# A recurrent attention and a bilinear network on one core: transposing keys and queries two slots at a time

## The chip, the core and the metric

The kernel runs on one core of a Trainium2 chip. The core has a matrix engine (TensorE, in the profile PE, with its weight loads as PEld), a vector engine (VectorE, DVE), a scalar engine (ScalarE, ACT), a general engine (GpSimd, POOL) and an engine that here only issues DMA transfers (SyncE, SP). Sixteen DMA engines move the data that they ask for. Each engine executes its own list of instructions in order and waits on semaphores for the others. The metric is the device time of one execution in microseconds; lower is better.

## What is computed

```python
def _attn_ref(q, k, v):                        # q, k, v: [4, 8, 768, 64] float32
    gamma = 1.0 - 2.0 ** (-5.0 - np.arange(H, dtype=np.float32))
    scale = 1.0 / np.sqrt(D)
    for t in range(S):
        state = gamma[None, :, None, None] * state + np.einsum('bhd,bhe->bhde', k[:, :, t], v[:, :, t])
        y[:, :, t] = scale * np.einsum('bhd,bhde->bhe', q[:, :, t], state)
...
    x = attn_out.transpose(0, 2, 1, 3).reshape(B * S, H * D)      # [3072, 512]
    a = x @ w_a                                # w_a, w_b: [512, 1536]
    b = x @ w_b
    return (a * b @ w_out)                     # w_out: [1536, 512]
```

A recurrence with a decay per head goes over 768 positions of 4 batches and 8 heads; its result, 3072 rows of 512, goes through two products whose outcomes are multiplied element by element and through a third product.

## The kernel before

**Slots.** The recurrence is worked in chunks of 128 positions, so that it becomes matrix products: inside a chunk, scores of queries against keys under a mask, and across chunks a state per head. One chunk of one batch, with all 8 heads, is a slot: 24 slots, numbered 0 to 23, 6 to a batch. Two neighbours (2u and 2u + 1) are a pair. The 3072 rows then go through the network in row groups of 4, 2, 2, 2, 2, 4 and 8 slots (`TILES`), whose index in the code is J.

**What happens to keys and queries.** The keys and queries of a slot are loaded in float32 (raw tiles `kf`, `qf`; values are `vf`), multiplied by a table that holds the decay, and written as bf16 into `kqb[t]`, a tile of 128 positions by 2 x 4 x 2 x 64 elements: first keys, then queries, 1,024 elements or 256 KB in all. `scaled` (L317 to L335) does one of the two halves in one instruction of 512 elements a partition. The state's products (L433) read keys from `kqb` as they are; scores (L415) and the products of queries with the state (L453) need them with the head's dimension on the partitions, as `kqT`.

**Two ways to `kqT`.** The first three pairs (slots 0 to 5) are transposed on TensorE (`flip2`, L524) and are worked by functions of their own (names that end in 2). The pairs from slot 6 on go through `flip`: a DMA transpose, issued by SP, from `kqb[t]` into one half of a tile `kqT` that belongs to the pair. There are 18 of these, of 256 KB each. In the later pairs the positions of a pair are interleaved: a score of either slot takes its keys from its own half of `kqT` and its queries from both halves (L416, L417).

**The order of the work.** `seq` (L103) chains the instructions of each engine in the order in which the program names them, so the order on each engine is the written one, and a wait holds up all that stands behind it on that engine. Semaphores between engines are put in by the framework, from the regions of the tiles that instructions read and write. A slot's preparation is `casts(t)` (L342): two scalings on GpSimd, the cast of the values where `t` isn't in 12 to 19, then on SP the transpose (L352) and, behind it, the loads for slot t + 2. For some slots the order of loads differs (L350 to L371): at t = 18 the keys and queries of slot 20 are loaded ahead of the transpose and the keys of 21 behind it. `casts_two` (L391) does this for slots 6 and 7, `late_kq` (L380) for the last four; `late_kq(20)` has the loads of slots 22 and 23 behind the two transposes. `turn(new, old)` (L477) is the attention's work on TensorE: the state and the scores of the pair `new`, the outputs of the pair `old`. Between turns TensorE works the network: `ffn_a` (L619) and `ffn_g` (L631) for the two first products, and the third product either directly (L656) or in seven products of half blocks in place of eight (`Group`, L717, with matmuls at L739). For the latter GpSimd or VectorE first forms sums of quarters of `ht` (`hsum`, L696, by the helper `tt` at L672): the tiles `hs` 1 to 4. `Group.p7` uses `hs` 3, `p6` uses `hs` 2, `p5` uses 1 and `p3` uses 4. `single(J)` (L835) works the seven products of row group J between the first blocks of the next one.

**The program around the change.** At the stretch that the prediction looks at longest, the written order is: `casts(13)`, `single(2)`, `casts(14)` with pieces of weight sums between its two scalings, blocks of row group 3, `casts(15)`, `hsum(3, 3, 0, 6)` on GpSimd, more blocks, `hsums(3, 0, 3)`, `turn(12, 10)`, blocks, `hsums(3, 3, 6)`, `casts(16)`, `single(3)`.

**Tiles.** The pool `nat` has 6 buffers of each of its tags. `kqb` is one of them: 6 slots are held at once, and the seventh waits for the readers of the first. When all slots are through, the same buffers take the sums `XS` of the last row group's input (`x_sum`, L881, on VectorE), four tiles of the same size: 3 and 2 are made first, later 1 and 4. `kqT` has 3 buffers of a pair. `load_slot` (L117) puts two slots' keys into one raw tile, and loads each slot's half by itself; for queries it loads both slots in one transfer at the even slot (L122).

Of the kernel before, what the change touches and what calls it, by code (L numbers as in the profile page):

```python
# [10 lines left out]
BF16 = mybir.dt.bfloat16  # L11
# [20 lines left out]
def kernel(  # L32
# [11 lines left out]
    P = 128  # L44
    B, H, S, D = q.shape
    NCH = S // P
    HP = H // 2
# [19 lines left out]
    nat = ctx.enter_context(tc.tile_pool(name="nat", bufs=6))  # L67
    tra = ctx.enter_context(tc.tile_pool(name="tra", bufs=4))
# [34 lines left out]
    def seq(bi):  # L103
        ins = bi.ins
        prev = last.get(ins.engine)
        if prev is not None:
            tc.add_manual_dep(ins, prev.name, nosync, reason="program order")
        last[ins.engine] = ins
        return bi
# [79 lines left out]
    kqb = {}  # L189
    kqb = {}  # L190
# [116 lines left out]
    kb, qb, vb, kqT, aT = {}, {}, {}, {}, {}  # L307
# [9 lines left out]
    def scaled(eng, t, i):  # L317
# [16 lines left out]
            tab = tab.rearrange("p (r hp) o -> p r hp o", r=2).to_broadcast([P, 2, HP, D])  # L334
        seq(eng.tensor_tensor(dst, src, tab, op=ALU.mult))  # L335

    def new_nat(t):
        kqb[t] = nat.tile([P, 2, HP, 2, D], BF16, tag="kqb", name="kqb")
        kb[t], qb[t] = kqb[t][:, 0], kqb[t][:, 1]
        vb[t] = nat.tile([P, H, D], BF16, tag="vb", name="vb")  # L340

    def casts(t, between=lambda: None):  # L342
        new_nat(t)
        scaled(nc.gpsimd, t, 0)
        between()
        scaled(nc.gpsimd, t, 1)
        if t not in range(12, 20):
            cast(nc.gpsimd, vb[t], raws["v", t])
        u = t + 2
        if u == 20:  # L350
            load_slot(u, "kq")
        flip(t)  # L352
        if u == 20:
            load_slot(u + 1, "k")
            return
        if u == 21:
            load_slot(u - 1, "v")
            load_slot(u, "v")
            load_slot(22, "kq")
            return  # L360
        if u in V_LATE:
            if u == 13:
                load_slot(12, "q")
            elif u == 19:
                load_slot(18, "kq")
            load_slot(u, {12: "k", 18: ""}.get(u, "kq"))
            if u % 2:
                load_slot(u - 1, "v")
                load_slot(u, "v")
        elif u < NSLOT:  # L370
            load_slot(u)  # L371

    def flip(t):
        if t % 2 == 0:
            kqT[t // 2] = tra.tile([P, 2, 2, HP, P], BF16, tag="kqT", name="kqT", bufs=3)
        seq(nc.sync.dma_start_transpose(
            out=kqT[t // 2][:, t % 2].rearrange("p a b c -> p (a b) c"),
            in_=kqb[t].rearrange("p a hp r d -> p (a hp r d)")))

    def late_kq(t):  # L380
        for u in (t, t + 1):
            new_nat(u)
            scaled(nc.gpsimd, u, 0)
            scaled(nc.gpsimd, u, 1)
            flip(u)
        if t == 20:
            load_slot(23, "k")
            load_slot(22, "v")
            load_slot(23, "v")

    def casts_two(t):  # L391
        for u in (t, t + 1):
            new_nat(u)
            scaled(nc.gpsimd, u, 0)
            scaled(nc.gpsimd, u, 1)
            flip(u)
        for u in (t, t + 1):
            cast(nc.gpsimd, vb[u], raws["v", u])
        load_slot(t + 3)
# [271 lines left out]
    def tt(dst, x, y, op, eng=nc.vector):  # L671
        seq(eng.tensor_tensor(dst, x, y, op=op))  # L672
# [175 lines left out]
    WS, XS, pieces = {}, {}, []  # L848
# [29 lines left out]
    def xq(k, c):  # L878
        return xt[BIG, c][:, 2 * k : 2 * k + 2]

    def x_sum(n):  # L881
        XS[n] = nat.tile([P, 2, 4 * P], BF16, tag="kqb", name=f"xs{n}")
        x, y, op = {3: (xq(1, 1), xq(0, 1), ALU.subtract), 2: (XS.get(3), xq(0, 0), ALU.add),
                    1: (xq(0, 1), xq(0, 0), ALU.subtract), 4: (xq(1, 0), XS.get(2), ALU.subtract)}[n]
        tt(XS[n], x, y, op)
# [191 lines left out]
    def big():  # L1077
        made = {"A": Group(5, 0, ST, AT0, FF), "B": Group(5, 1, FF, AT1, ST)}
        made.update({f"u{u}.": Unit(u) for u in range(2 * NP)})
        made.update(a=Group(BIG, 0, Y0, AT0, ST), b=Group(BIG, 1, Y1, AT1, FF),  # L1080
                    c=Group(BIG, 2, FF, AT0, ST, "kqT"), d=Group(BIG, 3, FF, AT1, FF, "kqT"))
        order = START.split()
        at = {7 * u + o: f"u{u}.{x}" for u in range(2, 2 * NP) for x, o in STEP.items()}
        at = [at[t] for t in sorted(at) if at[t] not in order]
        order += [x for x in at[: at.index(f"u{2 * NP - 1}.1")]] + END.split()
        for x in order:
            if x == "T":
                turn(None, 22)
            elif x[0] == "X":
                x_sum(int(x[1]))  # L1090
            elif x[0] == "S":
                hsum((BIG, int(x[1])), int(x[2]), 0, NP)
            elif x[-1] in "<>":
                made[x[:-2]].p1(*((0, NP - 1) if x[-1] == "<" else (NP - 1, NP)))
            else:
                getattr(made[x[:-1]], "p" + x[-1])()
# [226 lines left out]
```

## Time and profile before

| | |
|---|---|
| Median of 3 runs | 217.86 us (217.77 to 217.90) |
| Profiled execution | 218.26 us |
| its span | 216.6 us |
| GpSimd's two scalings of a slot | 1.04 us each (median of 40: 1,042 and 1,043 ns) |
| DMA transposes | 18, 4.5 us from issue to landing (median) |
| Key loads of one slot | 18 of 256 KB, 4.9 us from issue to landing (median) |
| Query loads of two slots | 9 of 512 KB, 5.8 us |
| Moved in all | 39.68 MB in 82,906 packets |

The span runs from the first to the last instruction that the profiler recorded; the execution's time is measured around it. A row of a timeline gives the start in us from the span's start, the length in us, the engine, the line of the code, the operation, the tile written and the tiles read, how many instructions were merged, and in brackets how long the engine had been idle and what ended that. For SP the length is the time that the queue was held by issuing the transfer; the transfer itself goes on behind it, and "to landing" counts from the start of the issue to the last piece of data that is in place. A row of the chain of waits has start, length, engine, tile and line. Engine names that end in q are an engine's queue.

### The profile page before, as it was taken

To read this page: it belongs to the slowest core of one execution; us is meant where nothing else is said; L and a number is where in the kernel's file an instruction comes from. 1 tells how busy PE (TensorE), PEld (TensorE's weight loads), DVE (VectorE), ACT (ScalarE), POOL (GpSimd) and SP (SyncE) were. 2 spreads that over 40 slices of the span, in tenths; PEclk is the share of its full clock that TensorE was granted. 3 is DMA by queue.
4 is the path that set the end of the run, shared out by engine and by line. 5 is a ranking of instruction groups with operands and counts; after the bars stand their busy time and mean duration, and the time that the engine had idled before them with its cause. 6 is when DMAs were issued, how large, how long until landed. Compare 5 with 4: busy or idle time off the path is not lost.

```text
span 216.6 us, 5726 instructions
## 1 busy us (share of the span) xinstructions
PE 209.8 (97%) x2250; PEld 145.8 (67%) x2250; DVE 151.1 (70%) x277; ACT 105.1 (49%) x236; POOL 155.5 (72%) x187
## 2 busy tenths in 40 slices
PE   7789999999999999999999999999999999999994
PEld 3458445587458888888888877557864444458883
DVE  5796347845985486356377978686577887688952
ACT  3175325343224444464576475657545656652331
POOL 7277877778889487979959979799996999530000
PEclk9999999999999999999999999999999999999999
DMA  6999999999999999399989999980013000000055
GB/s 181 315 337 370 377 360 357 363 237 240 227 267 235 173 254 280 76 189 257 213 187 227 222 200 215 236 139 3 5 73 122 0 0 3 2 0 0 27 194 170
DMA packets 82906, 39.68 MB, mean 183 GB/s; under 512 B 57536, under 2 KB 75840, under 8 KB 82880
## 3 DMA queue, kind: packets, MB, share of 16 engines
q1 hardware_dynamic: 82736, 39.26, 74.4%
q8 instruction: 17, 0.28, 0.5%
q10 hardware_dynamic: 144, 0.07, 0.1%
q14 instruction: 9, 0.07, 0.1%
HBM read 28.31 MB, written 6.29 MB: 160 GB/s over the span
## 4 chain that ended last, share of the span: by engine, by line
PE 91%; SPq 3%; DMA 3%; POOL 0%; issue 0%; DVE 0%
PE a L619 18%; PE g L631 18%; PE mA L739 12%; PE uA L913 10%; PE mB L739 6%; PE o L656 5%; PE uB L913 5%; DMA wsta<-in_moe_w_a_dram 3%; PE mC L739 3%; PE at L415 2%; PE uC L913 2%; SPq L150 2%; PE y L463 2%; PE st L433 2%; PE fa L1003 2%; SPq L138 1%
## 5 line engine op out<-in xcount | busy, mean ns | idle before, releaser
L633 DVE TENSOR_TENSOR ht<-g,asb 128x256 bf16<-128x256 f32 (+1 forms) x70 | 34.4, 493 | 30.3 <-PE g L631 27.1
L619 PE MATMUL a<-xt,wa_bf 128*128 128x256 bf16 (+1 forms) x280 | 48.6, 300 | 0.2 <-POOL wa_bf L287 0.2
L631 PE MATMUL g<-xt,wb_bf 128*128 128x256 bf16 (+1 forms) x280 | 48.4, 300 | 0.0
L622 ACT CAST asb<-a 128x256 bf16<-128x256 f32 (+1 forms) x70 | 30.0, 428 | 33.5 <-PE a L619 31.3
L631 PEld LDWEIGHTS <-wb_bf 128*128 128x128 bf16 x280 | 27.1, 98 | 10.2
L619 PEld LDWEIGHTS <-wa_bf 128*128 128x128 bf16 x280 | 26.5, 98 | 10.8 <-POOL wa_bf L287 0.6
L920 ACT COPY snap<-uA 128x512 f32<-128x512 f32 x36 | 20.0, 587 | 15.4 <-PE uA L913 13.9
L335 POOL TENSOR_TENSOR kqb<-kf,ktab 128x512 bf16<-128x512 f32 x22 | 22.9, 1045 | 5.3 <-DMA kf<-in_k_dram 4.9
L739 PEld LDWEIGHTS <-hs 128*128 128x128 bf16 x234 | 22.8, 98 | 3.6
L421 DVE TENSOR_TENSOR aT<-at,mask 128x512 bf16<-128x512 f32 x36 | 22.3, 683 | 0.3
L335 POOL TENSOR_TENSOR kqb<-qf,qtab 128x512 bf16<-128x512 f32 x18 | 19.8, 1100 | 2.6 <-DMA qf<-in_q_dram 1.6
L672 POOL TENSOR_TENSOR ht<-gsb,asb 128x512 bf16<-128x512 bf16 x13 | 15.2, 1174 | 7.5 <-DVE gsb L672 7.4
L746 ACT COPY snaps<-mA 128x256 f32<-128x256 f32 x30 | 11.0, 374 | 18.9 <-PE mA L739 18.9
L672 POOL TENSOR_TENSOR hs<-ht 128x384 bf16<-128x384 bf16 (+3 forms) x14 | 15.8, 1130 | 5.7 <-DMA kf<-in_k_dram 3.2
L739 PEld LDWEIGHTS <-ht 128*128 128x128 bf16 x180 | 17.5, 98 | 3.3
L672 POOL TENSOR_TENSOR hs<-ht,hs 128x384 bf16<-128x384 bf16 (+1 forms) x17 | 16.8, 993 | 2.5 <-DVE ht L633 2.3
L739 PE MATMUL mA<-wsum,hs 128*128 128x256 bf16 x120 | 15.2, 273 | 0.0
L672 DVE TENSOR_TENSOR osb<-mB,snaps 128x256 f32<-128x256 f32 x20 | 8.4, 422 | 8.2 <-ACT snaps L746 4.3
L287 POOL CAST vb<-vf 128x512 bf16<-128x512 f32 x12 | 7.8, 668 | 5.2 <-DMA vf<-in_v_dram 5.2
L656 PE MATMUL o<-wo_bf,ht 128*128 128x512 bf16 x48 | 10.7, 379 | 0.0
L672 DVE TENSOR_TENSOR gsb<-uB,snap 128x512 bf16<-128x512 f32 x12 | 8.2, 686 | 2.9 <-ACT snap L920 2.1
L672 DVE TENSOR_TENSOR asb<-uB,snap 128x512 bf16<-128x512 f32 x12 | 8.2, 685 | 2.9 <-ACT snap L920 2.0
(148 smaller groups left out, 379.8 us busy)
## 6 DMA issues: line engine op xcount, KB each, us to landing
out_dram<-osb SPq DMA_DIRECT2D x21, 256.0 KB, 3.9
kf<-in_k_dram SPq DMA_DIRECT2D x18, 256.0 KB, 4.9
qf<-in_q_dram SPq DMA_DIRECT2D x9, 512.0 KB, 5.8
vf<-in_v_dram SPq DMA_DIRECT2D x18, 256.0 KB, 5.1
wsta<-in_moe_w_a_dram SPq DMA_DIRECT2D x6, 512.0 KB, 7.2
wsto<-in_moe_w_out_dram SPq DMA_DIRECT2D x6, 512.0 KB, 8.7
wstb<-in_moe_w_b_dram SPq DMA_DIRECT2D x5, 512.0 KB, 7.9
kf<-in_k_dram SPq DMA_DIRECT2D x3, 512.0 KB, 7.4
```

Source lines behind the costliest of these rows:

```text
L335: seq(eng.tensor_tensor(dst, src, tab, op=ALU.mult))
L421: seq(nc.vector.tensor_tensor(aT[t][:, r], at[r], mask.to_broadcast([P, HP, P]), op=ALU.mult))
L619: seq(nc.tensor.matmul(a, wa_bf[:, kt, fs], xcols(J, kt, c0, c1), start=(kt == 0), stop=(kt == KT - 1)))
L622: seq(nc.scalar.copy(asb, a))
L631: seq(nc.tensor.matmul(g, wb_bf[:, kt, fs], xcols(J, kt, c0, c1), start=(kt == 0), stop=(kt == KT - 1)))
L633: seq(nc.vector.tensor_tensor(ht[J][:, ft, c0:c1], g, asbs.pop((J, ft, c0)), op=ALU.mult))
L656: seq(nc.tensor.matmul(o, ht[J][:, ft, i * P : (i + 1) * P], wo_bf[:, ft], start=(ft == 0), stop=(ft == NFT - 1), skip_group_check=True))
L672: seq(eng.tensor_tensor(dst, x, y, op=op))
L739: seq(nc.tensor.matmul(m, w, right[:, j], start=(first and j == 0), stop=(j == NP - 1), skip_group_check=True))
L746: seq(nc.scalar.copy(self.snaps[:, n], self.bank["A"]))
L913: seq(nc.tensor.matmul(m, w, right[:, k], start=(first and k == 0), stop=(k == 1), skip_group_check=True))
L920: seq(nc.scalar.copy(self.snaps[n], self.bank["A"]))
```

## The change

`kqb` becomes one tile for two neighbouring slots, allocated at the even slot, with 3 buffers in place of 6 of half the size; `kqb[t]` is then the slot's half of it, and what reads and writes it is unchanged. `flip` does nothing for an even slot. For the odd slot it issues one transpose of the whole pair, 128 positions by 2,048 elements, 512 KB, into the whole `kqT` tile. Slots 0 to 5 use the new tile too, but not `flip`. The four `XS` tiles become two tiles of two, in the same buffers.

```diff
+    both = {}
+
     def new_nat(t):
-        kqb[t] = nat.tile([P, 2, HP, 2, D], BF16, tag="kqb", name="kqb")
+        if t % 2 == 0:
+            both[t // 2] = nat.tile([P, 2, 2, HP, 2, D], BF16, tag="kqb", name="kqb", bufs=3)
+        kqb[t] = both[t // 2][:, t % 2]
         kb[t], qb[t] = kqb[t][:, 0], kqb[t][:, 1]
         vb[t] = nat.tile([P, H, D], BF16, tag="vb", name="vb")
...
     def flip(t):
         if t % 2 == 0:
-            kqT[t // 2] = tra.tile([P, 2, 2, HP, P], BF16, tag="kqT", name="kqT", bufs=3)
+            return
+        u = t // 2
+        kqT[u] = tra.tile([P, 2, 2, HP, P], BF16, tag="kqT", name="kqT", bufs=3)
         seq(nc.sync.dma_start_transpose(
-            out=kqT[t // 2][:, t % 2].rearrange("p a b c -> p (a b) c"),
-            in_=kqb[t].rearrange("p a hp r d -> p (a hp r d)")))
+            out=kqT[u].rearrange("p t a b c -> p (t a b) c"),
+            in_=both[u].rearrange("p t a hp r d -> p (t a hp r d)")))
...
     def x_sum(n):
-        XS[n] = nat.tile([P, 2, 4 * P], BF16, tag="kqb", name=f"xs{n}")
+        if n in (3, 1):
+            XS["pair"] = nat.tile([P, 2, 2, 4 * P], BF16, tag="kqb", name=f"xs{n}", bufs=3)
+        XS[n] = XS["pair"][:, int(n in (2, 4))]
```

## The prediction

> **What bounds the kernel now.** I read the page's busy times first, then the busy time by stages, then the transposes by themselves (when each is issued, when it lands, when TensorE first reads it), and last what GpSimd and the DMA queue wait for.
>
> ```profile
> span 216.6 us, 5726 instructions
> PE 209.8 (97%) x2250; PEld 145.8 (67%) x2250; DVE 151.1 (70%) x277; ACT 105.1 (49%) x236; POOL 155.5 (72%) x187
> ...
> 16.00:45.00 29.00, 28.82 (x299) 17.09 (x300) 17.87 (x30) 12.54 (x26) 22.31 (x31) 1.00 1.08 359
> 45.00:150.00 105.00, 104.98 (x1333) 80.67 (x1332) 73.03 (x137) 53.57 (x130) 88.08 (x96) 1.00 1.02 206
> 150.00:213.00 63.00, 63.00 (x442) 40.21 (x441) 48.02 (x78) 32.01 (x66) 36.17 (x37) 1.00 0.11 41
> ```
>
> The first two lines are the page's, the other three the busy time by stages (length, then PE, PEld, DVE, ACT, POOL, granted clock, DMA share, GB/s). From 16 to 213 us TensorE is idle for 0.18 + 0.02 + 0.00 = 0.20 us, at the full granted clock. All DMA transposes lie between 50 and 145 us, so inside a stretch in which TensorE never waits: whatever the change makes faster elsewhere can return 0.2 us at most, and whatever it makes TensorE wait for is added to the end in full, since the 63 us behind 150 have no idle time to give back.
>
> The profiled execution took 218.26 us, 1.66 more than its span; the median of the runs is 217.86, 0.40 less. I work out differences in the profiled execution and add them to 217.86.
>
> **What one transpose costs now.** All 18 together, then three stretches that hold two neighbours each (transposes of slots 6 and 7, 20 and 21, 22 and 23), and slots 16 and 17, each with its landing:
>
> ```profile
> L376 SPq DMA_TRANSPOSE kqT<-kqb x18: 1232/1332/3293, 50.3 to 141.0; - x18
> DMA to landing us min/median/max: 3.0/4.5/6.0
> ...
> L376 SPq DMA_TRANSPOSE kqT<-kqb x2: 1245/2269/3293, 50.3 to 53.7; - x2
> DMA to landing us min/median/max: 3.2/4.3/5.3
> ...
> L376 SPq DMA_TRANSPOSE kqT<-kqb x2: 1232/1232/1232, 105.9 to 108.0; - x2
> DMA to landing us min/median/max: 3.0/3.1/3.1
> ...
> L376 SPq DMA_TRANSPOSE kqT<-kqb x2: 1748/2261/2774, 130.1 to 132.9; - x2
> DMA to landing us min/median/max: 3.7/4.6/5.6
> ...
> L376 SPq DMA_TRANSPOSE kqT<-kqb x2: 1354/1781/2208, 138.4 to 141.0; - x2
> DMA to landing us min/median/max: 4.2/5.0/5.8
> ```
>
> The first row of a couple gives the time that SP is held by the instruction (ns, min/median/max), and the first and last start. Unhindered, 256 KB hold SP for 1.23 us and land 3.0 us after the start. In a backlog a second 256 KB lands 0.9 us behind the first (130.1 + 5.6 = 135.7, then 132.9 + 3.7 = 136.6). No row shows 512 KB in one transpose.
>
> **The change, part by part.**
>
> *Nine transposes go, nine double.* On SP it removes the transposes of the even slots and makes those of the odd slots cover both. The hold of SP for 512 KB lies between 1.23 us (it doesn't grow with size) and 2 x 1.23 = 2.46 us (it is all per byte); A plain load of 256 KB holds SP for 0.58 (row at 89.97 below); were that the fixed part of a transpose too, 512 KB would hold it for 0.58 + 2 x 0.65 = 1.88. I take 2.46, the price of the two instructions that the rows do show. The landing lies between 3.0 us after the start (the second half rides along) and 53.7 + 3.2 - 50.3 = 6.6 us (two, one behind the other, from the first's start); I take the odd slot's own landing plus 1.1, between the 0.9 of the backlog and the 1.23 of the hold.
>
> The Trainium skill, page "DMA: Bandwidth & Descriptors", section "Why a DMA increments its semaphore by 16 and not by 1", has a table by which generations before trn3 pushed a transpose tile by tile, so that its issue grows with its size. By that the hold is 2.46 and the stall found below is 0.32 in place of 0.19; the two equal holds of 1.23 above are one size only, and can't tell.
>
> *Does TensorE get the pair in time?* It needs both slots of a pair anyway: a score of either slot reads the queries of both (L417). So only the later transpose counted before, and nothing is lost by holding the earlier one back. The odd slots' issues on SP, then the first reads by TensorE (chain of waits):
>
> ```profile
> 63.28 2.10 SPq L376 DMA_TRANSPOSE kqT<-kqb  x1
> 71.95 1.25 SPq L376 DMA_TRANSPOSE kqT<-kqb  x1
> 88.69 1.23 SPq L376 DMA_TRANSPOSE kqT<-kqb  x1
> 89.97 0.58 SPq L129 DMA_DIRECT2D kf<-in_k_dram  x1
> 93.31 2.20 SPq L376 DMA_TRANSPOSE kqT<-kqb  x1
> 98.98 2.20 SPq L376 DMA_TRANSPOSE kqT<-kqb  x1
> 125.08 1.23 SPq L376 DMA_TRANSPOSE kqT<-kqb  x1
> ...
> 60.76 0.57 PE at L415 x32
> 76.15 0.55 PE at L415 x16
> 80.62 0.66 PE at L415 x32
> 96.74 0.57 PE at L415 x32
> 110.23 0.57 PE at L415 x32
> 116.27 0.66 PE at L415 x32
> 133.25 0.57 PE at L415 x32
> 140.27 0.57 PE at L415 x32
> 146.93 0.57 PE at L415 x32
> ```
>
> From issue to first read, pair by pair (issues of slots 7, 17, 21, 23 from the rows of couples): 60.76 - 53.7 = 7.1; 76.15 - 63.28 = 12.9; 8.7; 96.74 - 88.69 = 8.1; 11.3; 116.27 - 108.0 = 8.3; 8.2; 140.27 - 132.9 = 7.4; and for the last pair 146.93 - 141.0 = 5.9. Against the upper landing of 6.6 only the last pair is short, by 0.7 us; with the value I take, 4.2 + 1.1 = 5.3, it is 0.6 us early. So: nothing, at 0 to 0.7.
>
> *What stands behind the doubled transposes on SP.* The loads of an even slot's turn move up by the removed transpose (1.23 us or more), and those of an odd slot's turn move back by the growth of the one ahead of them, 0 to 1.23 us. Earlier loads end no wait of TensorE. Later ones matter where GpSimd waits for them and TensorE for GpSimd. GpSimd's work around two such places, and TensorE's weight loads behind the first:
>
> ```profile
> 87.62 1.04 POOL L335 TENSOR_TENSOR kqb<-qf,qtab 128x512 bf16<-128x512 f32 x1
> 88.62 1.04 POOL L335 TENSOR_TENSOR kqb<-kf,ktab 128x512 bf16<-128x512 f32 x1
> ...
> 94.91 1.04 POOL L335 TENSOR_TENSOR kqb<-kf,ktab 128x512 bf16<-128x512 f32 x1 [1.50 <-DMA kf<-in_k_dram]
> ...
> 100.36 1.78 POOL L672 TENSOR_TENSOR hs<-ht,hs 128x384 bf16<-128x384 bf16 x2
> ...
> 130.09 1.04 POOL L335 TENSOR_TENSOR kqb<-qf,qtab 128x512 bf16<-128x512 f32 x1
> ...
> 138.73 1.04 POOL L335 TENSOR_TENSOR kqb<-kf,ktab 128x512 bf16<-128x512 f32 x1 [1.11 <-DMA kf<-in_k_dram]
> ...
> 102.73 0.64 PEld L739 LDWEIGHTS <-hs 128*128 128x128 bf16 x6
> ```
>
> The key load of slot 15 (issue 89.97) stands right behind the transpose of slot 13 (88.69), which keeps its start, as GpSimd's scaling of slot 13 sets it (end 87.62 + 1.04 = 88.66). GpSimd waits 1.50 us for this load, then works without a gap: slot 15's two scalings, then the sums of ht (L672) for row group 3's product. The second of the two sums at 100.36 ends at 102.14; it is the second half of hs 2, and the weight loads of p6 need it from the fourth of six on, 102.73 + 3 x 0.107 = 103.05. The slack is 0.91 us. The load comes later by 0.9 (the data of 256 KB more ahead of it) to 1.23 (the hold); I take 1.1, so TensorE stalls 1.1 - 0.91 = 0.19 us, in a range of 0 to 0.32. (Below nothing isn't to be had: the start is GpSimd's, and more data stands ahead.) The sums behind it have the same lateness and later uses, so the stall is paid once.
>
> The key load of slot 23 (GpSimd waits until 138.73) stood behind the transposes of 20 and 21, issued from 130.1 to 132.9 + 1.75 = 134.7. The joint one can start when slot 21 is scaled, at 130.09 + 1.04 = 131.1, and is through at 133.6 (unhindered) to 134.7 (as before): the load comes up to 1 us earlier or where it was, and with it the last pair. Credit nothing.
>
> *Tiles.* kqb goes from 6 buffers of one slot to 3 of a pair. Slot 14's scaling now waits for the readers of slots 8 and 9 in place of 8 alone; both were read in the turn at 76.15, and the scaling of slot 14 begins at 88.62: 12 us of cover, and about as much for the others. The x sums (L882) take the same places in the same order. All at nothing; if the cover were gone, GpSimd would wait for the next turn.
>
> **Sum.** 9 x 1.23 us of SP's time saved at the even slots and 9 x 1.23 spent at the odd: 0 on the path. Last pair: 0. Slot 15's keys: +0.19. Span 216.6 + 0.19 = 216.8; beside the median, 217.86 + 0.19 = 218.05, say 218.1.
>
> **The rivals.**
>
> *All hidden.* The slack of 0.91 covers the later load, if the hold has a fixed part of 0.58 like a load's and the queue is empty: 217.86. Against: the data still stands ahead.
>
> *Slower: the joint transpose is blocked in its issue, and the keys of slot 15 come late.* The holds of 2.20 at 93.31 and 98.98 show that a transpose can wait 0.97 us longer in SP when others are under way; with twice as much to push, the one at 88.69 may meet this. Then it holds 2.46 + 0.97, the key load is 2.20 late, and TensorE stalls 2.20 - 0.91 = 1.29: 219.15. It decides from a lateness of 0.91 + 0.43 on. For: the hold grows with what is outstanding. Against: the two holds of exactly 1.23 at 105.9 and 108.0, and that of 88.69 itself, met no such wait.
>
> *Slower: the last pair is late.* Landing after 6.6 from 141.0 is 147.6, 0.67 after the first read: 218.53. For: it is the shortest lead, and landings reach 6.0 with half the data. Against: the queue ahead is short of loads there.
>
> *Faster.* Nine completions fewer and earlier loads give back idle time: 0.2 us at most by the stages, 217.66. More than 0.43 would need something no row shows. The Trainium skill's page "DMA: Bandwidth & Descriptors", section "Rules for kernel authors", tells to merge small transfers into one large; by it the time should fall, and here the rows cap that at 0.2.
>
> *It doesn't do what it says:* the 512 KB go out as two pieces back to back; then the hold is 2.46 and the figures are those of the forecast's upper end, 218.18.
>
> **How the numbers follow.** About 0.2% (0.43 us) is what a measurement of this kernel tells from no change. Forecast (stall 0.1 to 0.4) 0.44; all hidden 0.10; two pieces 0.02; these are "same": 0.56. Blocked issue 0.24 and last pair 0.14 are "slower": 0.38. Faster by over 0.2%: 0.06. The range goes from 217.6 (all of the 0.2 returned) to 219.2 (the blocked issue's price); a second wait of 0.97 on top is left out.
>
> **What would show it.** Right: nine transposes on SP with a hold near 2.46; TensorE's idle time between 16 and 213 us grown by 0.1 to 0.4, all of it ahead of the weight loads of hs near 103 us, with GpSimd's scaling of slot 15 about 1.1 us later than 94.91. Wrong: a gap ahead of the first reads of kqT (the last pair's above all), a hold far from 2.46, GpSimd waiting elsewhere, or TensorE as full as before and the end moved nonetheless.

## The result and the profile after

| | changed | before | ratio, 95% interval |
|---|---|---|---|
| first series, 7 runs each | 218.88 us | 217.90 us | 1.0048 (1.0027 to 1.0069) |
| again (e5), 12 and 35 runs | 218.57 us | 218.07 us | 1.0008 (0.9980 to 1.0036) |
| a third time (e10), 12 and 29 runs | 218.40 us | 218.28 us | 1.0006 (0.9996 to 1.0017) |

Times are medians. The ratios leave out executions in a slower state, which both kernels show now and then at a lower granted clock (0.976 in e10's longest, of 222.60 us), so they are not the quotients of the medians. The change is slower in the first series. In the two later ones the medians stand on the same side (+0.50 and +0.12 us) and the intervals include no change, though all 12 runs of e5 took 218.23 us or more. The first profile is of an execution of 219.82 us, the longest of its series, so it shows the loss at its largest. The page's first lines and the busy time by stages of the changed kernel (columns as before the change):

```profile
span 218.1 us, 5682 instructions
PE 209.4 (96%) x2238; PEld 145.7 (67%) x2250; DVE 150.4 (69%) x277; ACT 105.2 (48%) x236; POOL 156.1 (72%) x187
...
16.00:45.00 29.00, 28.64 (x299) 16.80 (x297) 16.69 (x28) 12.28 (x25) 21.57 (x30) 1.00 1.08 360
45.00:150.00 105.00, 103.26 (x1315) 79.33 (x1319) 72.02 (x135) 52.41 (x128) 85.87 (x94) 1.00 1.00 206
```

Between 45 and 150 us TensorE is now idle for 1.74 us, where it was idle for 0.02. (1.41 us of that is the wait shown next. The rest stands at no wait; 12 of the 2,250 matmul records are missing in this trace.) What TensorE waited for, in us in all, times, longest, and its rows around that place:

```profile
PE at L421 <- DMA kqT<-kqb: 1.4, 1, 1.4
...
140.23 0.64 PE L421 MATMUL at<-kqT 64*64 64x128 bf16 x32
...
145.93 1.03 PE L637 MATMUL g<-xt,wb_bf 128*128 128x512 bf16 x4
148.37 0.64 PE L421 MATMUL at<-kqT 64*64 64x128 bf16 x32 [1.41 <-DMA kqT<-kqb]
```

One wait, ahead of the first read of the last pair (slots 22 and 23). The same two reads in the kernel before:

```profile
140.20 0.64 PE L415 MATMUL at<-kqT 64*64 64x128 bf16 x32
146.86 0.64 PE L415 MATMUL at<-kqT 64*64 64x128 bf16 x32
```

From the first read of slots 20 and 21 to that of 22 and 23 it is 6.66 us before and 8.14 after: 1.48 us lost, all here, since at the first of these reads the two traces stand within 0.03 us of each other. In the other two profiles of the changed kernel the same distance is 7.84 (e5) and 6.92 (e10), so 1.18 and 0.26 lost: the place is the same each time and the size isn't.

**Where it comes from.** SP's rows of the changed kernel, then those of the kernel before that have not been shown:

```profile
125.12 3.03 SPq L382 DMA_TRANSPOSE kqT<-kqb  x1
128.26 1.16 SPq L129 DMA_DIRECT2D vf<-in_v_dram  x2
129.47 2.60 SPq L129 DMA_DIRECT2D kf<-in_k_dram  x1
132.12 1.03 SPq L138 DMA_DIRECT2D qf<-in_q_dram  x1
133.26 4.14 SPq L382 DMA_TRANSPOSE kqT<-kqb  x1
137.44 0.58 SPq L129 DMA_DIRECT2D kf<-in_k_dram  x1
...
144.06 1.76 SPq L382 DMA_TRANSPOSE kqT<-kqb  x1
```

```profile
119.87 2.63 SPq L376 DMA_TRANSPOSE kqT<-kqb  x1
...
127.67 1.28 SPq L129 DMA_DIRECT2D kf<-in_k_dram  x1
129.00 0.96 SPq L138 DMA_DIRECT2D qf<-in_q_dram  x1
130.06 4.62 SPq L376 DMA_TRANSPOSE kqT<-kqb  x2
134.74 0.57 SPq L129 DMA_DIRECT2D kf<-in_k_dram  x1
```

Read from the top: slot 18's 256 KB, issued at 119.87 before, now go out with slot 19's at 125.12, and that transpose holds SP for 3.03 us where slot 19's alone held it for 1.23 (+1.80). The key load of slot 22 behind it is held for 2.60 instead of 1.28 (+1.32). So the transposes of 20 and 21 begin 3.2 us later, at 133.26. Being one, they are 0.5 us quicker than the two were, and the key load of slot 23 behind them goes out at 137.44 instead of 134.74, 2.7 us late. These rows say where the time went and not which merged pair is to blame for the longer holds: e6 below shows that the pairs ahead of slot 18 have a part in them. GpSimd (its rows in the changed kernel) waits for that load:

```profile
95.89 1.04 POOL L335 TENSOR_TENSOR kqb<-kf,ktab 128x512 bf16<-128x512 f32 x1 [2.44 <-DMA kf<-in_k_dram]
...
101.35 1.78 POOL L678 TENSOR_TENSOR hs<-ht,hs 128x384 bf16<-128x384 bf16 x2
...
141.99 1.04 POOL L335 TENSOR_TENSOR kqb<-kf,ktab 128x512 bf16<-128x512 f32 x1 [3.33 <-DMA kf<-in_k_dram]
```

Slot 23 is scaled from 141.99, not 138.73; the last transpose starts at 144.06, not 141.0. All nine transposes, and the last one alone with its landing:

```profile
L382 SPq DMA_TRANSPOSE kqT<-kqb x9: 1671/3034/5332, 51.1 to 144.1; - x9
DMA to landing us min/median/max: 4.3/5.7/7.3
...
L382 SPq DMA_TRANSPOSE kqT<-kqb x1: 1761/1761/1761, 144.1 to 144.1; - x1
DMA to landing us min/median/max: 4.3/4.3/4.3
```

It lands 4.3 us after its issue; slot 23's 256 KB alone took 4.2. The lead of the last pair was 146.93 - 141.0 - 4.2 = 1.7 us; it starts 3.1 us late and takes 0.1 longer: 1.5 us are missing, the loss.

### The profile page after: what moved, and what is told of

The parts are those of the page before. It is cut to its first block, busy times and chain, and to the rows that moved or that the text cites. A ratio compares the mean times of both kernels' runs of the same rounds, so it can differ in the third digit from the quotient of the medians.

```text
span 218.1 us, 5682 instructions
## 1 busy us (share of the span) xinstructions
PE 209.4 (96%) x2238; PEld 145.7 (67%) x2250; DVE 150.4 (69%) x277; ACT 105.2 (48%) x236; POOL 156.1 (72%) x187
## 4 chain that ended last, share of the span: by engine, by line
PE 80%; DMA 8%; SPq 5%; issue 3%; POOL 2%; ACT 1%; DVE 0%; ACTq 0%; POOLq 0%
PE a L625 15%; PE g L637 15%; PE mA L745 12%; PE uA L921 9%; PE mB L745 6%; PE o L662 5%; PE uB L921 4%; DMA wsta<-in_moe_w_a_dram 3%; PE mC L745 3%; DMA qf<-in_q_dram 2%; PE uC L921 2%; DMA kqT<-kqb 2%; PE at L421 2%; SPq L150 2%; SPq L129 2%
## 5 line engine op out<-in xcount | busy, mean ns | idle before, releaser
L625 PE MATMUL a<-xt,wa_bf 128*128 128x256 bf16 (+1 forms) x277 | 48.4, 299 | 0.4 <-POOL wa_bf L287 0.2
L625 PEld LDWEIGHTS <-wa_bf 128*128 128x128 bf16 x280 | 26.5, 98 | 10.8 <-POOL wa_bf L287 0.5
L285 ACT CAST gst<-st 128x256 bf16<-128x256 f32 x14 | 5.2, 373 | 10.4 <-PE st L439 10.4
```

The lines of the kernel that those rows point to most:

```text
L625: seq(nc.tensor.matmul(a, wa_bf[:, kt, fs], xcols(J, kt, c0, c1), start=(kt == 0), stop=(kt == KT - 1)))
```

## The experiments

Two readings of this wait were to be told apart. Theory Q (queue): the key load of slot 23 stands on SP behind joint transposes and comes late, and everything behind it. Rival S (size): 512 KB in one piece land too late, whatever stands ahead. All have the kernel before on the same chip beside them; the changed kernel itself ran beside e6 to e8 (as e5) and beside e9 and e11 (as e10), but not beside e1 to e4, where the traces have to decide.

**e1: the key load moved ahead.** In `late_kq(20)` of the changed kernel:

```diff
             scaled(nc.gpsimd, u, 1)
+            if u == 21:
+                load_slot(23, "k")
             flip(u)
         if t == 20:
-            load_slot(23, "k")
             load_slot(22, "v")
```

> The changed kernel, with the key load of slot 23 issued on SP ahead of the joint transpose of slots 20 and 21 instead of behind it. Theory Q (queue: the key load of slot 23 stands behind joint transposes that hold SP, so slot 23 is scaled late and the last joint transpose is issued at 144.1 instead of 141.0): the key load is issued near 133.3 instead of 137.4, the last joint transpose near 141.0, it lands near 145.3, TensorE doesn't wait at its first read (146.9), time 217.8 to 218.1. Rival S (size: 512 KB in one piece land too late for the first read, whatever stands ahead): a stall of 0.5 us or more stays, 218.4 to 218.9. Rival W (the DMA engines have too much to move there, so the order on SP only passes the delay on): the transpose of slots 20 and 21 now lands after 140.2 and TensorE waits there, 0.2 to 0.8 us.

218.25 us against 218.13 (ratio 1.0010, 0.9985 to 1.0035). SP's rows, the scaling of slot 23's keys on GpSimd, the last transpose's landing and the first read:

```profile
132.17 1.33 SPq L129 DMA_DIRECT2D kf<-in_k_dram  x1
133.62 3.63 SPq L382 DMA_TRANSPOSE kqT<-kqb  x1
139.66 3.57 SPq L382 DMA_TRANSPOSE kqT<-kqb  x1
...
137.59 1.04 POOL L335 TENSOR_TENSOR kqb<-kf,ktab 128x512 bf16<-128x512 f32 x1
...
DMA to landing us min/median/max: 5.6/5.6/5.6
...
146.68 0.64 PE L422 MATMUL at<-kqT 64*64 64x128 bf16 x32
```

The load goes out 5.3 us earlier than in the changed kernel and GpSimd doesn't wait for it; the joint transpose starts at 139.66, lands at 145.3, and TensorE doesn't wait (no idle time stands at its row). Nine joint transposes of 512 KB are all still there. That contradicts S. The transposes of 20 and 21 are not late either (no wait at their read), so the order on SP didn't pass the delay on: they land at 133.62 + 5.6 = 139.2, and their first read is at 140.01.

**e2, e3, e4: one pair apart.** `flip` with an exception for one pair (9 in e2, 10 in e3, 11 in e4):

```diff
     def flip(t):
+        u = t // 2
+        if u in (9,):
+            if t % 2 == 0:
+                kqT[u] = tra.tile([P, 2, 2, HP, P], BF16, tag="kqT", name="kqT", bufs=3)
+            seq(nc.sync.dma_start_transpose(
+                out=kqT[u][:, t % 2].rearrange("p a b c -> p (a b) c"),
+                in_=kqb[t].rearrange("p a hp r d -> p (a hp r d)")))
+            return
         if t % 2 == 0:
             return
-        u = t // 2
```

> The changed kernel, with slots 18 and 19 transposed apart as before, all other pairs jointly. Theory Q, with the hold of SP by the joint transpose of 18 and 19 (3.03 us where the later of the two alone took 1.23) as its start: the key load of slot 23 is issued 1.5 us or more earlier than 137.4, the stall ahead of the last pair's first read falls from 1.5 to 0.3 us or less, time 217.8 to 218.2. Rival S (size of the last transpose): unchanged, 218.6 to 218.9.

> The changed kernel, with slots 20 and 21 transposed apart, all other pairs jointly. Both transposes stand at the same place of SP's queue, behind the loads of slot 22. Theory Q with its start at slots 18 and 19: the key load of slot 23 is issued at 137.4 within 0.5 us, the stall stays between 1.0 and 1.6, time 218.5 to 219.0. Theory Q with its start at the joint transpose of 20 and 21 itself: the load is issued 1 us or more earlier and the stall falls under 0.5, below 218.3. Rival S: unchanged, 218.6 to 218.9.

> The changed kernel, with slots 22 and 23 transposed apart, all other pairs jointly: the last transpose moves 256 KB and is still issued when slot 23 is scaled. Theory Q: it is issued near 144 and lands 3.0 to 4.2 us later, at 147.1 to 148.2; the stall stays between 0.3 and 1.4, time 218.2 to 218.8. Rival S: the stall goes, 217.8 to 218.0.

Against 218.13 us before, e2 took 218.15 (1.0005, 0.9985 to 1.0025), e3 218.50 (1.0010, 0.9990 to 1.0030), e4 218.75 (1.0024, 0.9997 to 1.0051). The key load of slot 23 and the last transpose in e2, then in e3:

```profile
135.40 0.58 SPq L129 DMA_DIRECT2D kf<-in_k_dram  x1
141.44 1.95 SPq L389 DMA_TRANSPOSE kqT<-kqb  x1
```

```profile
136.36 0.57 SPq L129 DMA_DIRECT2D kf<-in_k_dram  x1
142.30 2.06 SPq L389 DMA_TRANSPOSE kqT<-kqb  x1
```

In e2 no wait is left, as Q says for its start at 18 and 19. The load is out 2.0 us earlier, but this execution ran 0.8 us ahead (its first read of the last pair is at 146.06 and not 146.86), so it is 1.2 by the same clock, short of the 1.5 expected. e3 came between what it was to tell apart: the load is out 1.1 us earlier, and no wait is left in its profile, but the median stays 0.37 above, a difference that the interval doesn't tell from none. Taking either pair apart ends the wait in its profile, so the expectation of e3 that one of the two alone decides it was wrong. What e4's TensorE waits for, and its two last transposes:

```profile
PE mA L752 <- POOL hs L685: 0.2, 1, 0.2
...
L382 SPq DMA_TRANSPOSE kqT<-kqb x2: 1231/1624/2016, 140.8 to 143.2; - x2
DMA to landing us min/median/max: 3.2/3.9/4.6
```

With the last pair apart, slot 23's 256 KB start at 143.2 and land 3.2 us later at 146.4, ahead of the read: the small piece does win back what the late load cost there. In this Q was wrong: it had a wait of 0.3 to 1.4 us left at that read, and there is none. But the loss doesn't go, where S had expected it to. The late scaling of slot 23 holds up GpSimd's sums behind it, and the products that read them (at 151.4) wait instead: the products after these start at 152.65, 0.35 us later than in e3 (152.30), and the median is 0.62 above the kernel before, with an interval that just includes no change. So the late key load has two followers, the last transpose and the sums; S's remedy covers only one.

**e5, e10: the changed kernel again.**

> The changed kernel once more, on one chip with the next three. In its first profile TensorE waited 1.5 us ahead of the last pair's first read; that execution was its longest. If that wait is the whole loss, this profile shows a wait there that is equal to the excess of its span over 216.6 within 0.2 us, and the median is 0.5 to 1.2 us above the kernel before.

> The changed kernel, on one chip with the kernel with key load 23 moved. Theory Q: its median is 0.4 us or more above that of the next kernel.

The median rule held in e5, barely (+0.50). The rule on the span failed: TensorE waited 1.12 us, while the span of 217.3 is only 0.7 longer, since this execution reached the pair before already 0.5 us earlier (its row is at 139.68, not 140.20). The start of the program varies by such amounts (its first row of L625 begins at 15.57, the same products in the kernel before at 16.18); distances within one trace are the safer measure. e10's distance to e11 was 0.31 us, under the 0.4 expected. Its profile shows a second wait, on the weight loads of hs, which the other two lack:

```profile
102.98 0.32 PEld L745 LDWEIGHTS <-hs 128*128 128x128 bf16 x3
103.49 0.22 PEld L745 LDWEIGHTS <-hs 128*128 128x128 bf16 x3 [0.19 <-POOL hs L678]
```

**e6, e9: joint in one part only.** e6 has the exception for pairs 9, 10 and 11 (joint up to slot 17), e9 for all but 11 (joint only for the last).

> The changed kernel with slots 18 to 23 transposed apart as before, and the six pairs 6 to 17 jointly. Theory Q: the joint transposes of the early pairs cost nothing, the key load of slot 23 is issued near 134.7 as in the kernel before, no wait at the last pair: equal to the kernel before within 0.2%. If the early pairs cost something (slot 15's keys, 0 to 0.3 us), 0.1 to 0.3 us more, at the weight loads of hs near 103 us.

> The changed kernel with only the last pair transposed jointly, slots 6 to 21 apart as before, so that what stands ahead of slot 23's key load on SP is as before and only the last transpose is large. Theory Q: the joint transpose is issued near 141.0, lands near 145.3, TensorE doesn't wait at the last pair's first read: equal to the kernel before within 0.2%. Rival S: a wait of 0.5 us or more there, 218.4 or more.

e6: 218.10 against 218.07 (0.9996, 0.9972 to 1.0020); six joint transposes of the early pairs cost no time. But the key load of slot 23 did not go out near 134.7. Its row in e6, and the first read of slots 20 and 21:

```profile
136.04 0.57 SPq L129 DMA_DIRECT2D kf<-in_k_dram  x1
...
139.69 0.64 PE L428 MATMUL at<-kqT 64*64 64x128 bf16 x32
```

From the load to that read it is 3.65 us, where the kernel before has 140.20 - 134.74 = 5.46. So the load is 1.8 us late with no joint transpose from slot 18 on; TensorE doesn't wait, as the slack of the last pair still covers it. The same distance is 5.24 in e9, 4.00 in e2, 3.86 in e3, 3.46 in e10, and 2.75 to 2.79 in e5 and the first profile of the changed kernel. A wait at the last pair shows only in the last three: 0.19 us in e10, and 1.12 and 1.41 in the two with the shortest distance. By these traces, one of each run, the lateness gathers along the queue from the early pairs on; how much each pair adds was not separated.

e9: 218.22 against 218.28 (0.9999, 0.9988 to 1.0009). Its SP rows, the landing, the first read and the stage:

```profile
134.97 0.57 SPq L129 DMA_DIRECT2D kf<-in_k_dram  x1
141.36 1.69 SPq L389 DMA_TRANSPOSE kqT<-kqb  x1
...
DMA to landing us min/median/max: 4.3/4.3/4.3
...
146.87 0.64 PE L428 MATMUL at<-kqT 64*64 64x128 bf16 x32
...
45.00:150.00 105.00, 104.98 (x1334) 80.67 (x1332) 70.48 (x137) 53.56 (x130) 87.21 (x96) 1.00 1.03 206
```

This is the sharpest test of S: the last 512 KB go out in one piece, the load ahead is in time, and TensorE is as full as before the change. They land at 141.36 + 4.3 = 145.7, 1.2 us ahead of the read.

**e7, e8: the load's place in the kernel before.** No joint transposes; the key load of slot 23 ahead of the transposes of 20 and 21 (e7), or behind the value loads (e8, whose edit this is):

```diff
         if t == 20:
-            load_slot(23, "k")
             load_slot(22, "v")
             load_slot(23, "v")
+            load_slot(23, "k")
```

> The kernel before, with all 18 transposes, and the key load of slot 23 issued ahead of the transposes of slots 20 and 21. Theory Q: TensorE has no idle time to return there, so equal to the kernel before within 0.2%; the key load lands some 3 us earlier and the transpose of slot 23 is issued near 139.

> The kernel before, with all 18 transposes of 256 KB, and the key load of slot 23 issued behind the value loads of slots 22 and 23 instead of ahead of them: the suspected cause alone, without a joint transpose. Theory Q: the load lands 1.5 to 2.5 us later than 138.7, the transpose of slot 23 is issued as much later, and what exceeds the lead of 1.7 us is lost: 0 to 0.8 us at the last pair's first read or at the products that wait for GpSimd's sums behind slot 23; time 218.0 to 218.8. Rival S (512 KB in one piece): nothing, within 0.2% of the kernel before.

e7: 218.34 against 218.07 (1.0017, 0.9985 to 1.0049), no difference shown, as expected; the transpose of slot 23 went out at 140.1 and not near 139. e8: 219.04 against 218.07 (1.0040, 1.0006 to 1.0073), more than expected. The load, GpSimd and TensorE's waits in e8:

```profile
136.37 0.92 SPq L129 DMA_DIRECT2D kf<-in_k_dram  x1
...
142.24 1.04 POOL L335 TENSOR_TENSOR kqb<-kf,ktab 128x512 bf16<-128x512 f32 x1 [4.69 <-DMA kf<-in_k_dram]
...
PE mA L739 <- POOL hs L672: 0.8, 1, 0.8
PE at L415 <- DMA kqT<-kqb: 0.6, 1, 0.6
```

With 18 transposes of 256 KB, the late load alone makes a loss of the changed kernel's kind: GpSimd starts slot 23 at 142.24, 3.5 us late, and TensorE waits at the last pair (0.6) and at the sums (0.8). The load is issued 1.6 us later than in the kernel before, and with the value loads now ahead of it it also takes 5.8 us to land instead of 3.9. Six of its twelve executions lie at 218.06 to 218.38 and six at 219.70 to 220.30; the profile is of an upper one, so for the lower half no loss is shown. What decides between the two was not found.

**e11: the moved load again, beside the changed kernel.**

> The changed kernel with the key load of slot 23 ahead of the joint transpose of slots 20 and 21, on one chip with the changed kernel. Theory Q: 0.4 us or more below the changed kernel's median, and within 0.2% of the kernel before.

218.09 against 218.40 for the changed kernel and 218.28 for the kernel before (0.9997, 0.9974 to 1.0019). The direction is Q's, the distance less than expected, and the single runs of e10 and e11 overlap, so the times alone don't show it. The profile does: the load goes out at 132.68, the last transpose at 140.93, and TensorE doesn't wait at the last pair. None of the versions beats the kernel before: TensorE has nothing to return.

## Why the prediction was right or wrong

- **The bound.** Right. TensorE had 0.20 us to give, no version came out faster beyond its interval, and each wait that the change made was added to the end.
- **The time.** Forecast 218.1, measured 218.88, in the range of 217.6 to 219.2; the likeliest case (a difference within 0.2%) was not what the first series gave. That the time lies in the range is luck: the 0.19 us forecast at the weight loads of hs didn't make the loss, and the loss that came arose at a step credited with nothing. It is the gap ahead of the last pair's first read that the prediction had named as a sign of being wrong. The rival of the right place was "the last pair is late" (218.53), and its mechanism, a landing of 6.6 us, was not the right one: the last pair landed 4.3 us after its issue (the forecast took 5.3), and the issue was 3.1 us late.
- **The hold for 512 KB.** Taken as 2.46 us, wrong as a size: the shortest are 1.67 to 1.76 (e9: 1.69, so 0.46 more than for 256 KB), and at slot 13 it was 2.02 although SP had issued nothing for 6 us. But what counted was the hold behind other transfers: 3.03, 4.14, up to 5.33. The Trainium skill's table of transposes ("DMA: Bandwidth & Descriptors", section "Why a DMA increments its semaphore by 16 and not by 1"), by which the issue grows with the size, is borne out in its direction: 1.69 for 1.23. A doubling is not seen.
- **Slot 15's keys.** The lateness was right: forecast 1.1 us, measured 95.89 - 94.91 = 0.98, with the second half of hs 2 ready at 103.13 instead of 102.14. The stall of 0.19 us, the one term of the sum, was too large. A wait is in one of three profiles (e10: 0.19 on the weight loads, the sums there at 101.65 + 1.78 = 103.43), and of that the products lost 0.08: the next ones start 103.83 - 103.09 = 0.74 us after them, against 103.49 - 102.83 = 0.66 before. In the other two the slack covered it.
- **Slot 23's keys.** This step failed: "the load comes up to 1 us earlier or where it was, and with it the last pair. Credit nothing." The joint transpose was held to start when slot 21 is scaled, at 131.1. It started at 133.26, as the loads of slot 22 ahead of it on SP had themselves been pushed back by the transpose of 18 and 19 and, as e6 shows, by the pairs before. I added up what each doubled transpose does to the load behind it, and not what it does to the next transpose and, through that, to the load after. The traces of e1, e11 and e8 show it from both sides: with the load early the wait goes, with the load late it comes without any joint transpose.
- **The blocked issue.** Priced at the transpose of slot 13, where the hold was 2.02 and not 3.43, and nothing was lost; the long holds that cost were those further on, of 18 to 21.
- **Merging as such.** The Trainium skill's advice to merge small transfers ("DMA: Bandwidth & Descriptors", section "Rules for kernel authors") brought nothing here: six merged pairs in e6 leave the time where it was, nine in the changed kernel raise it. The same section of the Trainium skill says that under 64 KB one pays mostly overhead. The transfers here were of 256 KB, so the prediction stretched the rule in applying it to them.
- **Tiles.** Nothing seen: TensorE waits at no other place that the change touches, and e6 and e9, which use the paired tiles throughout, equal the kernel before.

## What to carry to other kernels

Merging two transfers doesn't only save an issue: it moves the first one's bytes to the second one's time, and what is queued behind pays. Follow a late issue along the queue past the next load to the one whose consumer has the shortest lead, and count the delays of all merged transfers ahead of it, the early ones too. When a queue carries both results and loads, the load with the shortest lead belongs ahead of the large transfer; in e1 and e11 that one line of order took the wait away.

## What the hardware showed that was not expected

In e9 the one transpose of 512 KB held SP for 1.69 us and landed 4.3 us after its start, against 1.23 and 3.0 for 256 KB at the shortest: the hold is 0.5 us longer, the landing 1.3. Right behind other transfers, holds reached 5.33 us, and a plain 256 KB load behind a joint transpose was held for 2.60 (1.28 before). The long holds stand where other transfers had just been issued; that what is outstanding makes them long fits this and was not tested, nor how much may be outstanding before they grow.
